# Talking-heads attention and FNet mixing on one core: a new timetable for the mixing stage, and two small copies on another engine

## The chip, the cores and the metric

The kernel runs on one core of one Trainium2 chip. The core has TensorE (in profiles PE, and PEld for its weight loads), VectorE (DVE), ScalarE (ACT), GpSimd (POOL) and SyncE (SP), which issues transfers alone; 16 DMA engines carry the transfers of all queues. What counts is the device time of one launch, in microseconds; the median of several runs is given.

## The reference

Eight batches, twelve heads, 448 rows of 64 numbers a head, all in fp32. Attention comes first, with two small matrices that mix the heads, one before the softmax and one after it:

```python
scores = scale * np.matmul(q, k.transpose(0, 1, 3, 2))
scores = np.einsum('bhij,hg->bgij', scores, w_pre)
scores = scores - np.max(scores, axis=-1, keepdims=True)
attn = np.exp(scores)
attn = attn / (np.sum(attn, axis=-1, keepdims=True) + 1e-09)
attn = np.einsum('bhij,hg->bgij', attn, w_post)
out = np.matmul(attn, v)                        # to x: (8, 448, 768)
X = np.fft.fft(np.fft.fft(x, axis=1), axis=2)
u = x + np.real(X)
un = (u - mean(u)) / np.sqrt(var(u) + 1e-06)    # over the last axis
y = u + np.maximum(un @ w_ch1, 0.0) @ w_ch2     # 768 -> 3072 -> 768
```

## The kernel before

There are two stages: the mixing stage (`mix_phase`), which takes the first 850 us or so and ends with u in device memory, and the dense stage (`ffn_phase`), which normalises u and multiplies it by the two weight matrices. The change lies in the mixing stage alone. The dense stage starts with work of the first batch while the last transform products of the last batch are still open (`parts`).

**Steps.** The rows of a batch are cut into eight blocks (`BLOCKS`), and a block into 3 steps (one has 2), 23 steps a batch (`GS`), 184 in all. In a step twenty rows of all twelve heads go through the softmax. Its work is spread over time: the gather of step T (L493), four transfers on SP that bring rows of scores from the tile Sb into the tile Kr, is written out four steps ahead of T; the product that mixes heads ahead of the softmax, *premix* (L504, out of Kr into the PSUM tiles mx0 and mx1), the maxima (L511, VectorE), the exponentials (L518, ScalarE, out of mx into PP), the reciprocal (L525, L526) and the scaling (L528, POOL) two steps ahead; the product that mixes heads after it, *postmix* (L538, into po), and its transposition, *turn* (L551, VectorE, into Pv), in step T itself. mx0 and mx1 have one buffer each, Kr and PP three.

**Products that fill the steps.** Beside these fixed parts TensorE has other products, which a timetable spreads over the steps:

- T: transposition of q or k for a third of the heads (L450); Tq0 is that of q's third 0. It needs two score banks, emptied by ScalarE and VectorE, one each.
- QK: the scores of one block, for a third of the heads (L476); QK3.1 is block 3, third 1. Two banks, emptied by ScalarE into Sb (L342).
- AV: attention times v for two blocks (a group of rows) and a third of the heads (L568). Two banks, emptied by ScalarE into the tile XT (L342), in four small copies each.
- X: transposition of a group's result (L612), two banks, emptied by ScalarE into the tile X; X0 to X3 are the four groups.
- z: four products of the transform along rows (L677), z0 to z3, one bank each, ScalarE.
- s: four products of the transform along columns (L693), s00, s01, s10, s11 (pair of groups, parity), one bank each; VectorE adds each to X in four additions (L704, L706). After s01 and s11 the pair's rows are stored: by an indirect transfer that POOL issues (L716) and by plain ones on SP (L722, L724). L722 writes into the same tensor as the indirect one and waits until that has landed.

The score banks are a ring of four PSUM tiles, ms (`pms`, L336), shared by all products of the list; mx has two banks and po two. Between X and z lie the *folds* (L633 to L655), twenty pieces of elementwise work a batch on POOL, of which one or two are dealt out in a step.

**Rows that straddle.** Two groups of rows don't end where the transform's groups end, so a few columns of XT are copied to another group's XT (`SPILL`, L594): 15 columns of group 3 to group 1, 7 of group 2 to group 3, for six pieces each. This is done straight after the last eviction of an AV (inside `done`), and X of the receiving group has to wait for it. In the kernel before, POOL makes these copies.

**The timetable.** The constants `AT_*` say in which step of a batch (counted from the batch's first, so over 22 means during the next batch) a product is due: AT_T for T, by third of heads and q or k, counted one batch back; AT_QK for QK, counted from 7 steps ahead of the block; AT_AV for AV, counted from the group's last step plus one; AT_X, AT_Z and AT_S for X, z and s. AT_L and AT_V are the steps of the loads of q, k and v, which POOL issues; the loads of q and k are given out in the order in which the transpositions are due. Below, *place* is the number of a step within a batch, 0 to 22, and T, z, s and X of another batch are meant where the batch in question has none due at that place.

**Order within a step.** The main loop (L808 to L840) takes the parts of a step in one of two written orders, the first in even steps and the second in odd ones; as 23 is odd, a place has the other order in the next batch.

```python
ORDERS = tuple(o.split() for o in (
    "conv pre post flush AV max0 exp0 "
    "QK max1 exp1 turn scale full gather",
    "pre post flush max0 max1 QK exp0 "
    "AV turn exp1 scale gather conv full flush"))
```

`full` takes T, X, z and s; `conv` is one step of the conversion of weights for the dense stage (VectorE); `flush` writes out the evictions that are pending. Where a QK or AV would bring more than four pending evictions, and ahead of each product of `full`, they are flushed first. The order on TensorE, VectorE, ScalarE and POOL is kept as written (`manual_schedule`); each engine works through its queue in that order. Only SP's queue is put in order by the scheduler.

Of the kernel before, what the change touches and what calls it, by code (L numbers as in the profile page):

```python
# [85 lines left out]

AT_T = ((5, 9), (16, 17), (13, 15))
AT_L = ((-4, -3), (-2, -1), (0, 1), (2, 7), (11, 12), (13, 14))  # L90
AT_V = ((3, 4), (5, 6), (7, 7))
AT_QK = ((1, 2, 2), (0, 1, 2), (0, 1, 2), (1, 1, 2),
         (0, 1, 2), (0, 1, 2), (0, 1, 2), (0, 1, 2))
AT_AV = ((1, 2, 3), (0, 1, 5), (3, 4, 5), (1, 2, 4))
AT_X = ((11, 0), (23, 1), (28, 3), (30, 2))
AT_Z = (39, 39, 41, 41)
AT_S = ((40, 44), (46, 50))

ORDERS = tuple(o.split() for o in (
    "conv pre post flush AV max0 exp0 "  # L100
# [47 lines left out]
def _ap(t: bass.AP, offset: int, dims) -> bass.AP:  # L148
    return bass.AP(tensor=t.tensor, offset=t.offset + offset,
                   ap=[list(d) for d in dims])  # L150
# [6 lines left out]
def _row(t: bass.AP) -> int:  # L157
    return t.ap[0][0]
# [144 lines left out]
def mix_phase(ctx, tc, rest, ident, q, k, v, w_pre, w_post, u_scr, u_rev, wts):  # L303
# [6 lines left out]
    nc = tc.nc  # L310
# [30 lines left out]
    def copy(eng, out, in_):  # L341
        (nc.scalar.copy if eng == "a" else nc.vector.tensor_copy)(out=out, in_=in_)  # L342
# [11 lines left out]
    def ms_tile():  # L354
        return ms[-1]()
# [41 lines left out]
    first = {}  # L397
    START = sorted(range(3), key=lambda xx: max(AT_T[xx]))
    blocks = [dict(b=n // NBL, r0=BLOCKS[n % NBL][0], rs=BLOCKS[n % NBL][1])
# [7 lines left out]
    def emit_load_qk(b, xx, nm, y):  # L407

        src = q if nm == "q" else k
        if y == 0 and b == 0 and xx == START[-1]:  # L410

            if "raw" not in first:
                first["raw"] = ppv.tile([P, GT, 2 * S], F32, name="Pv", tag="Pv")
            batches[b]["raw" + nm, xx] = first["raw"][:, nm == "q"].rearrange(
                "p (c x d) -> p c x d", c=C7, x=2)
        elif y == 0:
            batches[b]["raw" + nm, xx] = praw.tile([P, C7, 2, D], F32, name="raw" + nm,
                                                   tag="raw")
        t = batches[b]["raw" + nm, xx]
        for x in range(2):  # L420
            eng = nc.gpsimd if b else (nc.sync, nc.scalar)[x]
            eng.dma_start(
                out=t[64 * y:64 * y + 64, :, x, :],
                in_=src[b, 6 * y + 2 * xx + x].rearrange("(p c) d -> p c d", c=C7))
        return True
# [36 lines left out]
    def emit_qk(n, xx):  # L462

        bk = blocks[n]
        st = batches[bk["b"]]
        if "Sb" not in bk:
            bk["Sb"] = psb.tile([P, 6, S], F32, name="Sb", tag="Sb")
        c0, w = bk["r0"] + MG, R * bk["rs"]
        n = 64 + w
        pss = [ms_tile() for _ in range(2)]  # L470
        for y in range(2):
            for o in (64 * y, 64 * y + 32):
                lo = c0 + o - 64 + (0 if y else w)
                hi = min(lo + 32, c0 + w)
                for x in range(2):
                    nc.tensor.matmul(  # L476
                        pss[x][o:o + hi - lo, :S],
                        st["qT", xx][64 * x:64 * x + 64, y, lo:hi],
                        st["kT", xx][64 * x:64 * x + 64, y, :],
                        start=True, stop=True)  # L480
        return [lambda x=x: copy(ENG["QK"][x], bk["Sb"][:n, 2 * xx + x, :],
                                 pss[x][:n, :S]) for x in range(2)]
# [73 lines left out]
    def emit_av(a, pr):  # L556

        b, k = divmod(a, NG)
        st = batches[b]
        Pv = turned[a]["Pv"]  # L560
        rp = _row(Pv)
        nu = (GROUP_AT[k + 1] - GROUP_AT[k]) * 4
        pss = [ms_tile() for _ in range(2)]
        for jb in range(C7):
            for x in range(2):
                for y in range(2):
                    i = 2 * pr + x
                    nc.tensor.matmul(  # L568
                        pss[y][64 * x:64 * x + 64, :nu * R],
                        st["v", pr][64 * y:64 * y + 64, x, jb * D:(jb + 1) * D],  # L570
                        _ap(Pv, 64 * y * rp + 32 * jb + R * i,
                            [[rp, 64], [HS, nu], [1, R]]),
                        start=(jb == 0), stop=(jb == C7 - 1))
        g = groups[b * NG + BLOCKS[2 * k][3]]
        if pr == 0:
            g["XT"] = pxt.tile([P, 6, XW], F32, name="XT", tag="XT")
        XT = g["XT"]
        rx = _row(XT)

        def done(y):  # L580
            rs = _row(pss[y])
            c = 0
            for _, w, n, _, first, sg in BLOCKS[2 * k:2 * k + 2]:
                dst = _ap(XT, (3 * y + pr) * XW + PG[g["gi"]] + first,
                          [[rx, P], [sg * w, R], [sg, w]])
                src = _ap(pss[y], c, [[rs, P], [1, R], [R, w]])
                copy(ENG["AV"][y], dst, src)
                c += R * w
            if y == 1 and pr == 2:
                if k in SPILL:  # L590
                    gi, c0, n, go, co = SPILL[k]
                    Xo = groups[b * NG + go]["XT"]
                    back = -1 if gi == 2 else 1
                    nc.gpsimd.tensor_copy(  # L594
                        out=_ap(Xo, PG[go] + co, [[rx, P], [XW, 6], [1 - 2 * (go == 1), n]]),
                        in_=_ap(XT, PG[gi] + c0, [[rx, P], [XW, 6], [back, n]]))
                if k in NONE:
                    gi, cols = NONE[k]
                    for o in cols:
                        Xo = groups[b * NG + gi]["XT"]  # L600
                        nc.vector.memset(Xo[:, :, PG[gi] + o:PG[gi] + o + 1], 0.0)
        return [lambda y=y: done(y) for y in range(2)]

    def emit_x(g):
        X = pxx.tile([PN, DM], F32, name="X", tag="X")
        XT, p0 = g.pop("XT"), PG[g["gi"]]
        g["X"] = X
        evs = []
        for u in range(2):
            ps = ms_tile()  # L610
            for i in range(3):
                nc.tensor.transpose(ps[:PN, i * P:(i + 1) * P],  # L612
                                    XT[:, 3 * u + i, p0:p0 + PN], ident[:, :])
            evs.append(lambda u=u, ps=ps: copy(ENG["X"][u], X[:, u * DH:(u + 1) * DH],
                                               ps[:PN, :DH]))
        if g["gi"] in (1, 2):
            fold(g)
        return evs
# [113 lines left out]
    def due(kind, at, fn):  # L732
        fill[kind].append((at, len(fill[kind]), fn))
# [4 lines left out]
    for b in range(B):  # L738
        f = b * GS
        at_t = [(a, nm, xx) for xx, at in enumerate(AT_T) for nm, a in zip("qk", at)]  # L740
        if b == 0:
# [11 lines left out]
        else:  # L753
            for at, (a, nm, xx) in zip(AT_L, sorted(at_t, key=lambda e: e[0])):
                for y in range(2):
                    due("none", f + at[y] - GS,
                        lambda b=b, xx=xx, nm=nm, y=y: emit_load_qk(b, xx, nm, y))
            for xx, at in enumerate(AT_T):
                for nm, a in zip("qk", at):
# [5 lines left out]
        for n in range(0 if b else 2, NBL):  # L765
            for xx in range(3):
                due("QK", f + BLOCK_AT[n] - 7 + AT_QK[n][xx],
                    lambda n=NBL * b + n, xx=xx: (emit_qk(n, xx), n))
        for n in range(NG):
            for pr in range(3):  # L770
                due("AV", f + GROUP_AT[n + 1] + AT_AV[n][pr],
                    lambda a=b * NG + n, pr=pr: (emit_av(a, pr), None))
            at, gi = AT_X[n]
            due("full", f + at, lambda g=groups[b * NG + gi]: emit_x(g))
        for n, at in enumerate(AT_Z):
            due("full", f + at, lambda b=b, n=n: emit_z(b, n // 2, n % 2))
        for pair in range(2):
            for par in range(2):
                due("full", f + AT_S[pair][par],
                    lambda b=b, pair=pair, par=par: emit_s2(b, pair, par))  # L780
# [26 lines left out]
    with tc.manual_schedule(engines={ET.PE, ET.DVE, ET.Activation, ET.Pool}):  # L807
        while s <= TOT - GS + AT_X[-1][0]:  # L808
            old = len(later)
# [592 lines left out]
```

## Time and profile before

| what | value |
|---|---|
| time, median of 3 runs | 2429.42 us (2429.25 to 2429.75) |
| the profiled execution: its own time, its span | 2420.56 us, 2418.7 us |
| TensorE busy, whole span | 2307.4 us, 95% |
| VectorE, ScalarE, GpSimd busy, whole span | 71%, 46%, 47% |
| premix (L504), postmix (L538), QK (L476), busy | 234.6, 211.3, 208.5 us |
| AV (L568), busy | 161.7 us |
| maxima (L511), exponentials (L518), scaling (L528), busy | 215.2, 230.6, 239.3 us |
| the straddling copies on POOL (L594) | 16, of 0.255 us at the median |
| from 840 to 910 us, between the stages | TensorE idle for about half of it |

The busy time of TensorE is that of overlapping instructions with modelled ends, so it says how little is idle, not how near the engine is to its peak. More is told by the waits, and by the distance from one group of products to the next on TensorE's timeline: a group that comes at the usual distance was not held up. fp32 products show twice in the records (16 for the eight of a premix). A wait is put down to the semaphore that came last.

### The profile page before, as it was taken

The numbers are of one execution on the slowest core, as the hardware profiler recorded it, in microseconds if no ns is written. First come the engines' busy times: TensorE is split into PE (matmuls) and PEld (weight loads), VectorE is DVE, ScalarE is ACT, GpSimd is POOL, SyncE is SP. The second block draws the span as 40 slices with busy tenths as digits, with TensorE's granted clock in tenths as the row PEclk, the third lists the DMA queues.
The fourth block names the chain that finished last, engine by engine and source line by source line (L and its number), as shares of the span: only waits on it lengthen the run. The fifth ranks groups of instructions, "written<-read, shape, count | busy, mean of one in ns | idle before, by whom it ended". The sixth has DMA issues, their size and how long they took to land.

```text
span 2418.7 us, 59291 instructions
## 1 busy us (share of the span) xinstructions
PE 2307.4 (95%) x22600; PEld 1726.4 (71%) x22600; DVE 1706.3 (71%) x3596; ACT 1106.3 (46%) x3069; POOL 1133.5 (47%) x1684
## 2 busy tenths in 40 slices
PE   6999999999999949999999999999999999999998
PEld 3445454554545437676777779999899999999998
DVE  3878778777877735778576776777776777776546
ACT  4766666665666622323122224344444444444444
POOL 3577867766785651121043344333433343344333
PEclk9999999999999979999999999999999999999999
DMA  7555555645554473574887895657565756575553
GB/s 164 162 163 168 164 161 154 178 151 166 172 167 138 155 237 126 177 230 167 307 206 223 243 277 159 181 145 240 151 168 148 227 151 188 144 220 126 144 124 66
DMA packets 213384, 425.59 MB, mean 176 GB/s; under 512 B 38766, under 2 KB 135430, under 8 KB 213102
## 3 DMA queue, kind: packets, MB, share of 16 engines
q1 hardware_dynamic: 142446, 280.38, 33.4%
q0 software_dynamic: 64656, 139.45, 26.6%
q8 instruction: 181, 2.97, 0.5%
q10 hardware_dynamic: 6000, 1.97, 0.4%
q14 instruction: 101, 0.83, 0.1%
HBM read 213.16 MB, written 129.39 MB: 142 GB/s over the span
## 4 chain that ended last, share of the span: by engine, by line
PE 73%; issue 7%; DVE 6%; POOL 6%; DMA 4%; ACT 3%; SPq 1%; ACTq 0%; POOLq 0%; DVEq 0%
PE psP L1058 15%; PE psP L1188 10%; PE psR L1058 8%; PE mx L504 5%; PE psR L1188 5%; PE ms L568 5%; PE psQ L1058 4%; PE psP L1131 4%; PE ms L476 4%; PE po L538 4%; PE psQ L1188 2%; DMA Kr<-Sb 2%; PE psR L1131 2%; PE ms L693 2%; ACT PP L518 1%
## 5 line engine op out<-in xcount | busy, mean ns | idle before, releaser
L1058 PE MATMUL psP<-ub,w1t 128*128 128x256 f32 x2016 | 480.5, 379 | 1.2 <-DVE h L1077 1.2
L1058 PEld LDWEIGHTS psP<-ub,w1t 128*128 128x128 f32 x2016 | 379.0, 190 | 49.5 <-DVE h L1077 1.6
L528 POOL TENSOR_SCALAR PP<-PP,rcp 128x448 f32<-128x448 f32 x368 | 239.3, 659 | 255.7 <-DVE rcp L526 218.6
L518 ACT ACTIVATE PP<-mx,nmx 128x448 f32<-128x448 f32 x368 | 230.6, 631 | 217.9 <-DVE nmx L511 203.8
L511 DVE TENSOR_REDUCE nmx<-mx 128x1 f32<-128x448 f32 x368 | 215.2, 618 | 104.0 <-PE mx L504 101.5
L1222 POOL DMA_DIRECT2D out_dram<-od x109 | 132.9, 1394 | 280.0 <-DVE od L1219 157.6
L504 PE MATMUL mx<-Kr,kw 60*32 60x448 f32 x2944 | 234.6, 559 | 22.2 <-ACT PP L518 13.0
L1022 POOL TENSOR_TENSOR hq<-h 128x256 f32<-128x256 f32 (+1 forms) x168 | 104.1, 620 | 295.3 <-ACT h L1078 174.1
L1058 PE MATMUL psR<-ub,w1t 128*128 128x256 f32 x1008 | 232.5, 380 | 0.0
L1219 DVE TENSOR_TENSOR od<-od 128x768 f32<-128x768 f32 x196 | 188.9, 975 | 52.4 <-ACT od L1216 50.6
L476 PE MATMUL ms<-kT,qT 64*32 64x448 f32 (+2 forms) x3072 | 208.5, 544 | 8.3 <-ACT qT L342 6.3
L538 PE MATMUL po<-PP,kw 60*32 60x448 f32 x2944 | 211.3, 542 | 1.4 <-POOL PP L528 1.4
L1058 PEld LDWEIGHTS psR<-ub,w1t 128*128 128x128 f32 x1008 | 192.4, 191 | 26.3
L551 DVE STREAM_TRANSPOSE Pv<-po 128x896 f32<-128x896 f32 x184 | 203.9, 1108 | 9.9 <-PE po L538 7.8
L342 ACT COPY Sb<-ms 124x448 f32<-124x448 f32 (+1 forms) x384 | 184.5, 540 | 27.8 <-PE ms L476 22.6
L1216 ACT COPY od<-psP 128x192 f32<-128x192 f32 x390 | 124.7, 320 | 145.8 <-PE psP L1188 141.3
L568 PEld LDWEIGHTS ms<-Pv,vv 64*64 64x64 f32 x5376 | 138.4, 132 | 71.1 <-issue 47.9
L225 POOL DMA_DIRECT2D raw<-in_moe_w_ch_dram x88 | 53.5, 608 | 270.6 <-DVE tmp L269 253.3
L568 PE MATMUL ms<-Pv,vv 64*64 64x120 f32 (+1 forms) x5376 | 161.7, 263 | 0.8 <-issue 0.6
L1131 PE MATMUL psP<-w2t,h 128*128 128x384 f32 x448 | 153.7, 486 | 0.0
L504 PEld LDWEIGHTS mx<-Kr,kw 60*32 60x32 f32 x2944 | 48.1, 106 | 124.1 <-ACT PP L518 74.3
L1077 DVE TENSOR_TENSOR h<-h,psP 128x512 f32<-128x512 f32 x42 | 28.9, 687 | 143.4 <-PE psP L1058 143.1
(142 smaller groups left out, 4577.5 us busy)
## 6 DMA issues: line engine op xcount, KB each, us to landing
ub<-ub SPq DMA_DIRECT2D x294, 384.0 KB
Kr<-Sb SPq DMA_DIRECT2D x736, 105.0 KB
out_dram<-od POOLq DMA_DIRECT2D x137, 384.0 KB, 7.8
w1t<-w SPq DMA_DIRECT2D x42, 384.0 KB
w2t<-w SPq DMA_DIRECT2D x42, 384.0 KB
raw<-in_moe_w_ch_dram POOLq DMA_DIRECT2D x56, 256.0 KB, 3.8
raw<-in_moe_w_ch_dram POOLq DMA_DIRECT2D x32, 384.0 KB, 4.9
w<-wst POOLq DMA_DIRECT2D x92, 128.0 KB, 4.6
```

The lines of the kernel that those rows point to most:

```text
L476: nc.tensor.matmul(pss[x][o:o + hi - lo, :S], st["qT", xx][64 * x:64 * x + 64, y, lo:hi], st["kT", xx][64 * x:64 * x + 64, y, :], start=Tr ...
L504: nc.tensor.matmul(mx[x][64 * z + o:64 * z + o + 32, :S], kw1[64 * x:64 * x + KR, o:o + 32], Kr[64 * x:64 * x + KR, z, :], start=True, sto ...
L511: nc.vector.tensor_reduce(nmx[:, :], steps[T]["mx"][x][:, :S], axis=AX.X, op=ALU.max, negate=True)
L518: nc.scalar.activation(steps[T]["PP"][:, x, :], steps[T]["mx"][x][:, :S], ACTF.Exp, bias=steps[T]["nmx", x][:, :], accum_out=steps[T]["den ...
L528: nc.gpsimd.tensor_scalar(PP[:, x, :], PP[:, x, :], rcp[:, x:x + 1], 1.0, op0=ALU.mult, op1=ALU.mult)
L538: nc.tensor.matmul(po[o:o + 32, z, :S], kw2[64 * z:64 * z + KR, y, :], PP[64 * z:64 * z + KR, :, c * HS:(c + 1) * HS], start=True, stop=True)
L551: nc.vector.transpose(turned[a]["Pv"][:, j, :].rearrange("p (z s) -> p z s", z=2), steps[T]["po"][:, :, :S])
L568: nc.tensor.matmul(pss[y][64 * x:64 * x + 64, :nu * R], st["v", pr][64 * y:64 * y + 64, x, jb * D:(jb + 1) * D], _ap(Pv, 64 * y * rp + 32 ...
L1058: nc.tensor.matmul(p[:, m, :], w1[i][:, kc, m * P:(m + 1) * P], ub[:, kc, :], start=i in (0, 4, 1)[:3 - seed] and m == kc == 0, stop=kc == ...
L1131: nc.tensor.matmul(p, h[:, LHS[i], kf, x * P:(x + 1) * P], w2[i][:, kf, :], start=i in (0, 4, 1)[:3 - (c > 0)] and kf == 0, stop=kf == FM ...
L1188: nc.tensor.matmul(ps[j, key][:, :DQ], a, b, start=m in (0, 4), stop=True, skip_group_check=True)
L1219: eng.tensor_tensor(D[j][:, :, :], D[j][:, :, :], D[k][:, :, :], op=ALU.add)
```

## The change

The timetable gets other numbers, and ScalarE makes the straddling copies instead of POOL. Nothing is computed otherwise, and the number of products, copies and transfers stays the same. By place within a batch, the moves are:

- QK3.1 from 2 to 3; s11 from 4 to 3; X2 from 7 to 6
- AV0.2 from 9 to 10; X0 from 11 to 13; AV1.2 from 16 to 14; Tq1 from 16 to 15
- QK0.0 of the next batch from 17 to 16, QK0.2 of it from 18 to 17 (QK0.1 stays at 18)
- AV2.0 from 20 to 18, AV2.1 from 21 to 20; z2 and z3 from 18 to 19
- the loads of q's third 1 and of k's third 2 change places (2 and 7 against 11 and 12), as their transpositions do
- the loop has one step less after the last batch, as it ends with X2

On SP the row store L722 of pair 1 stands two gathers' worth of steps earlier in every second batch (before the gather for place 10 of the even batches, where it was before that for place 12), and at the same point in the others. In the last batches' tail s11 comes ahead of AV3.2 instead of behind it.

```diff
-AT_T = ((5, 9), (16, 17), (13, 15))
+AT_T = ((5, 9), (15, 17), (13, 15))
 AT_L = ((-4, -3), (-2, -1), (0, 1), (2, 7), (11, 12), (13, 14))
 AT_V = ((3, 4), (5, 6), (7, 7))
-AT_QK = ((1, 2, 2), (0, 1, 2), (0, 1, 2), (1, 1, 2),
+AT_QK = ((0, 2, 1), (0, 1, 2), (0, 1, 2), (1, 2, 2),
          (0, 1, 2), (0, 1, 2), (0, 1, 2), (0, 1, 2))
-AT_AV = ((1, 2, 3), (0, 1, 5), (3, 4, 5), (1, 2, 4))
-AT_X = ((11, 0), (23, 1), (28, 3), (30, 2))
-AT_Z = (39, 39, 41, 41)
-AT_S = ((40, 44), (46, 50))
+AT_AV = ((1, 2, 4), (0, 1, 3), (1, 3, 5), (1, 2, 4))
+AT_X = ((13, 0), (23, 1), (28, 3), (29, 2))
+AT_Z = (39, 39, 42, 42)
+AT_S = ((40, 44), (46, 49))
...
-                    nc.gpsimd.tensor_copy(
+                    nc.scalar.copy(
                         out=_ap(Xo, PG[go] + co, [[rx, P], [XW, 6], [1 - 2 * (go == 1), n]]),
                         in_=_ap(XT, PG[gi] + c0, [[rx, P], [XW, 6], [back, n]]))
```

## The prediction

> **What bounds the kernel now.** I read the page first: all edits lie in the mixing stage, the first 850 us of the span of 2418.7 us. Then the busy time of two whole batches of 23 steps, one whose first step takes the even order of work (batch 2) and one that takes the odd (batch 3); columns: length, then PE, PEld, DVE, ACT, POOL busy (instructions), clock, DMA share, GB/s.
>
> ```profile
> 232.31:335.94 103.63, 99.33 (x1926) 54.37 (x1926) 80.01 (x166) 68.18 (x206) 79.23 (x123) 1.00 0.53 163
> 335.94:441.81 105.87, 100.25 (x1931) 54.12 (x1919) 82.36 (x164) 68.32 (x209) 76.67 (x119) 1.00 0.54 163
> ```
>
> TensorE is busy 95% of it, and its work is the same after the change; so only its waits can go or come. Their list for 60 to 860 us (total, times, longest):
>
> ```profile
> PE mx L504 <- ACT PP L518: 12.1, 19, 2.6
> PE ms L612 <- POOL XT L594: 11.1, 10, 2.7
> PE ms L677 <- ACT Sb L342: 4.6, 6, 1.0
> PE ms L450 <- ACT Sb L342: 3.7, 3, 1.4
> PE mx L504 <- DMA Kr<-Sb: 3.1, 6, 1.2
> ```
>
> The first is the softmax chain in steps that hold too few products; the second is the copy that the change moves; the next two are score banks not yet emptied; the last is a gather. The timeline of PE shows where. A step runs from one premix (L504, 16 records) to the next, and undisturbed groups follow each other at fixed distances: premix 0.78, postmix 0.75 (0.89 ahead of an AV), QK 0.75 to 0.9, AV 1.63 (1.4 if short), a transposition 0.9, an s product 1.4 to 1.5. Lines of three places in batches 2 and 3:
>
> ```profile
> 296.66 0.96 PE L476 MATMUL ms<-kT,qT 64*32 64x448 f32 x16
> 298.67 1.24 PE L504 MATMUL mx<-Kr,kw 60*32 60x448 f32 x12 [1.05 <-ACT PP L518]
> ...
> 317.42 1.79 PE L677 MATMUL ms<-ts,xf 112*96 112x113 f32 x16 [0.89 <-ACT Sb L342]
> ...
> 363.08 0.91 PE L612 MATMUL ms<-ident,XT 128*113 128x128 f32 x6 [0.54 <-POOL XT L594]
> 365.40 0.98 PE L450 MATMUL ms<-ident,rawq 128*128 128x128 f32 x7 [1.41 <-ACT Sb L342]
> ```
>
> Place 14 (one QK only) waits 1.05 for the exponentials. Place 18 (two QKs, then z2 and z3) waits 0.89 for the first QK's bank. Place 5 waits for the copy, then 1.41 more for a bank: had the copy been early, the bank would have held it as long. VectorE tells why that bank was late: the four additions of s11 stood ahead of the maxima.
>
> ```profile
> 361.56 0.55 DVE L706 TENSOR_TENSOR X<-X,ms 113x383 f32<-113x383 f32 x1
> 362.03 0.92 DVE L273 TENSOR_TENSOR wst<-wst,tmp 128x256 f32<-128x256 f32 x1
> 362.88 1.14 DVE L511 TENSOR_REDUCE nmx<-mx 128x1 f32<-128x448 f32 x2
> ```
>
> **What the Trainium skill says.** Its page "PSUM — Partial Sum Buffer" (Specifications) gives 8 banks a partition, of 512 fp32 values. The kernel takes two for mx, two for po, four for ms: the ring of four can't grow, and the trace shows its waits (4.6 + 3.7 us). "Perfetto Trace Analysis" (Tensor Engine Instruction) says that ACT, DVE and GPSIMD are strict FIFO; the POOL copy, behind scalings, folds and loads, agrees: its own 0.26 us is preceded by PE waits of up to 2.7. "DMA: Bandwidth & Descriptors" (Issuing engines are not separate DMA queues) says all queues share 16 engines; the trace has a gather on the chain that took 7.18 us from 268.05, while V and k loads ran.
>
> **The change part by part.** Step lengths before are from PE's timeline of batch 2 / 3.
>
> *Copies.* 16 copies leave POOL (0.26 us at the median) for ScalarE, straight behind the evictions that they read. No row shows that form; bounds are 0.20 (128x40, XT) and 0.50 (113x384, X). On the line between 128x60 (0.226) and 113x384 (0.495) 90 and 42 elements cost 0.25 and 0.21: 0.46 a batch, hidden in ScalarE's 35% idle time; uncovered it would be 3.7 us over 8 batches. Queued behind the copy are evictions of a QK or exponentials, 0.25 late, and VectorE's memset of the same tile (L601), with the maxima behind it. VectorE spends 3.2 us a step (two maxima 1.24, turn 1.11, reciprocal 0.34, a weight conversion some 0.5), so steps of over 4 us cover that. Gained: in odd batches the wait ahead of X1 at place 0 (1.0 in batches 3 and 5, 0.4 in batch 1), all of it; at place 5 next to nothing (bank), but in batch 7, which has no transposition there, 2 to 3.
>
> *Places 2 to 7* (QK3.1 from 2 to 3; s11 from 4 to 3; X2 from 7 to 6). Before: 4.83+3.05+6.35+5.41+3.05+5.95 = 28.6 / 5.25+2.66+6.16+6.25+2.52+5.93 = 28.8. After: 2 and 4 become QK+AV (4.05 to 4.65 in their like: 4.1, 4.5), 3 two QKs with s11: 4.66 of work plus a bank wait as at place 18 (0.7) = 5.4; 5 stays 5.3, the additions being gone and the bank wait not; 6 becomes 3.4, X2 filling a light step; 7 is QK+AV, 4.6. Sum 27.3: gain 1.3 / 1.5.
>
> *Places 9 to 21* (AV0.2 to 10, X0 to 13, AV1.2 to 14, Tq1 to 15, QK0.0 to 16, QK0.2 to 17, AV2.0 to 18, z2 and z3 to 19, AV2.1 to 20). Before 57.6 in batch 2 and 58.9 in batch 3. After: 9 is 4.2 (its gather stays late: it is issued on the eviction of QK4.2, and steps 7 and 8 are now 8.7 instead of 10), 10 and 11 4.5, 12 3.8, 13 and 15 5.1 each (4.2 of work, 0.9 for QK's bank), 14 4.3, 16 and 19 4.4, 17 4.7, 18 4.5, 20 4.6, 21 4.1: 58.2: 0.6 lost in batch 2, 0.7 gained in 3. The waits of light steps become bank waits. Of the dearer cases of batches 4 to 6 (place 14 5.13, 15 5.32, 9 6.77 and 8.31) I count half as saved, by my choice: steps of over 4 us cover VectorE. Two waits are new. Tq1 at 15 clears its pads on POOL (L444, L445, 0.1 each) once QK7.2 of that step has read the old buffer; scalings stand behind them, needed two steps later: free. QK0.0's eviction at 16 overwrites the scores of block 6, one step earlier than before, so it waits for the last gather from them; that is issued behind the premix of place 14, takes SP 3.2 and lands some 2 later, some 4 us ahead of the eviction: free.
>
> *Loads and queues.* q1 and k2 change places in POOL's loads: k2 now has 3 steps (13 us) from issue to use; such loads land in 2.7 to 5.7 us. Free. In even batches the stores of pair 1 are issued two steps earlier; on SP the row store L722, which waits 2.5 to 4.6 us for the indirect store, stands before the gather of place 8 instead of 10. The gathers behind it are late by that; they were issued some 8 us ahead of their use, so I take 0, bounds 0 and 2 us in three batches.
>
> *Sum.* Even batches: 1.3 - 0.6, and 0.3 at place 1 (4.6 becomes 4.3), 1.0 x 3; half of what 4 and 6 take more than 2 (106.5 and 105.2 against 103.6), 2.2: 5.2. Odd: 1.5 + 0.7 + 1.0 (copy) = 3.2 in batch 3; 4.4 in 5 (half of the 2.4 that it takes more); batch 1, which has neither s10 nor s11, 2.5 in the same way (27.4 - 25.2 at 2 to 7, -0.1 at 9 to 21, 0.4 copy): 10.1. Batch 0, AVs moved alone: 1, estimated. Batch 7: 3 at place 5. Tail: the last s11 (861.16) moves ahead of one of three AVs (4.95 us together): 1.6; the store that begins at 864.27 heads the chain to the second stage's loads. Total 20.9; I round it down to 20, as new waits are likelier to be missed than new gains. Against the profiled execution's span: 2418.7 - 20 = 2398.7. It took 2420.56, and the median is 2429.42, 8.9 above; the same step gives **2409.4**.
>
> **Rivals.** *Better:* all light-step waits go and the banks cost nothing: 0.9 less at places 3, 13 and 15 in 7 batches, 19 more: 2390. For: 12.1 us of waits for exponentials. Against: place 18's wait shows in all six batches.
> *Nothing:* places 2 to 7 give only 0.5, and dear batches stay dear: 7 x 0.5 = 3.5, copies and tail 2.4 + 2.5 + 1.6: about 2419; with gathers late by 2 us in three even batches 2425. For: the place-by-place sum of 9 to 21, near nothing.
> *Slower, by the ring of four ms banks:* places 3, 13 and 15 each ask for more than four banks, so the last product waits for a QK eviction behind both exponentials. I priced this 0.7 to 0.9. Place 5, built alike, ran 6.25 to 7.27 in odd batches with 4.1 of work. If each of the three costs 1.5 more than priced, 31 us are lost in 7 batches: 2440. It decides from 0.95 more (20/7/3). Against: place 5 had VectorE late by s11, and 13 and 15 have no additions; but 15 gives VectorE 1.67 us of evictions, and 17 follows with 2.2 of additions and 0.55.
>
> **How the numbers follow.** Forecast (2400 to 2420) 0.55; better 0.12; nothing 0.15; slower 0.18. Within 0.2% is 2424.6 to 2434.3, about what a measurement of this kernel can tell from no change. Of "nothing" half is faster than that; of "slower" a sixth lies inside. Faster 0.55+0.12+0.07 = 0.74, same 0.11, slower 0.15. Range 2394 to 2436: it leaves out most of the slower case and the end of the better one; the forecast's own range is 2400 to 2420.
>
> **What would show it.** Right: no PE wait on POOL XT; place 14 over 4 us with no wait for PP; place 13 near 5.1 with T waiting for Sb; batches of 101 to 104 us; the store of the tail at about 862 minus the stage's gain. Wrong: place 3, 13 or 15 above 6; premix at place 8 or 9 waiting for Kr in every even batch; VectorE behind at 18, so that premix waits for PP there.

## The result, and the profile after

| | median | runs |
|---|---|---|
| before | 2429.34 us | 6 runs, 2420.45 to 2430.75 |
| after | 2389.08 us | 6 runs, 2381.97 to 2394.12 |

The ratio is 0.9836, interval 0.9814 to 0.9858: 40 us less, twice the forecast of 20 and 5 us below the range. Single slow executions (of the kernel before 2488.72 us, and of one variant 9237.21) are left out of every ratio below. The profiled execution took 2391.53 us, with a span of 2389.8. TensorE's busy time stays near what it was (2291.4 us; 2307.4 before). The same two batches as in the prediction, from the first premix of each to the next (columns as there: length, PE, PEld, DVE, ACT, POOL, clock, DMA share, GB/s):

```profile
229.44:328.97 99.53, 97.02 (x1926) 53.65 (x1926) 85.15 (x166) 66.67 (x207) 78.88 (x121) 0.98 0.56 169
328.97:430.97 102.00, 97.28 (x1931) 52.58 (x1919) 81.05 (x164) 67.50 (x211) 76.40 (x118) 0.98 0.57 169
```

They are 4.1 and 3.9 us shorter than before. PE's busy time fell by 2.3 and 3.0 of that, with the same work, so some of what counted as busy had been waiting. And the clock is 0.98, where it was 1.00: there is something new in them. PE's waits from 60 to 860 us (one of 19.5 us that belongs to the dense stage is left out):

```profile
PE mx L504 <- DMA Kr<-Sb: 9.9, 8, 3.2
PE mx L504 <- ACT PP L518: 6.6, 5, 2.0
PE ms L450 <- ACT Sb L342: 5.2, 13, 1.4
PE ms L693 <- ACT Sb L342: 1.9, 6, 0.3
PE ms L612 <- ACT XT L594: 0.8, 1, 0.8
```

The copy's wait went (11.1 to 0.8), as forecast, and the waits for score banks are small. The wait for a gather grew from 3.1 to 9.9 us, which was not forecast. PE's timeline has the places that the prediction showed: 13, with X0 and two transpositions behind one QK; 18 to 20 of batch 2; 5 of batch 3.

```profile
289.19 0.91 PE L612 MATMUL ms<-ident,XT 128*113 128x128 f32 x6
290.34 0.98 PE L450 MATMUL ms<-ident,rawq 128*128 128x128 f32 x7 [0.23 <-ACT Sb L342]
...
316.89 0.98 PE L504 MATMUL mx<-Kr,kw 60*32 60x448 f32 x16
317.67 0.96 PE L538 MATMUL po<-PP,kw 60*32 60x448 f32 x16
318.56 1.71 PE L568 MATMUL ms<-Pv,vv 64*64 64x120 f32 x56
320.20 0.98 PE L476 MATMUL ms<-kT,qT 64*32 64x448 f32 x16
320.98 0.96 PE L504 MATMUL mx<-Kr,kw 60*32 60x448 f32 x16
...
355.44 0.98 PE L450 MATMUL ms<-ident,rawq 128*128 128x128 f32 x7 [0.63 <-ACT Sb L342]
```

The bank at place 13 costs 0.23 where 0.9 was priced; place 5 keeps half of its bank wait. Place 20 (316.89 to 320.98), with one QK and one AV, is 4.09 long, the plain sum of its four groups: 0.78 + 0.89 + 1.64 + 0.78. The step of the same kind before the change, which had served as the price, looked like this on PE's timeline of batch 2:

```profile
321.66 1.20 PE L504 MATMUL mx<-Kr,kw 60*32 60x448 f32 x12
322.49 0.60 PE L538 MATMUL po<-PP,kw 60*32 60x448 f32 x4
322.68 0.56 PE L504 MATMUL mx<-Kr,kw 60*32 60x448 f32 x4
322.86 1.12 PE L538 MATMUL po<-PP,kw 60*32 60x448 f32 x12
323.91 1.70 PE L568 MATMUL ms<-Pv,vv 64*64 64x120 f32 x56
325.54 0.98 PE L476 MATMUL ms<-kT,qT 64*32 64x448 f32 x16
326.32 0.96 PE L504 MATMUL mx<-Kr,kw 60*32 60x448 f32 x16
```

It is 4.66 long, and no wait is printed. Yet from the first premix record to the AV it takes 2.25 us, where after it takes 1.67: the premix comes in pieces (12 records, then 4 between those of the postmix) behind a step of 2.52. The trace has the reason on ScalarE: the exponentials of the step before end at 321.51 and 322.13, and the premix, which overwrites both banks, starts the records of its two halves at 321.66 and 322.28. A light step's wait had gone into the length of the next one.

The new stalls are two. In batches 3 and 5 place 9 takes 9.33 and 11.12 us, where its groups alone make 3.3 (as in batch 6 of the variant with the row stored apart, 3.31). "Place 9's gather" is the one that brings the rows which the premix at place 9 reads. PE's lines in batch 3, and SP's queue at that time:

```profile
367.71 0.94 PE L504 MATMUL mx<-Kr,kw 60*32 60x448 f32 x4
371.86 1.82 PE L504 MATMUL mx<-Kr,kw 60*32 60x448 f32 x10 [3.21 <-DMA Kr<-Sb]
```

```profile
351.00 7.15 SPq L493 DMA_DIRECT2D Kr<-Sb  x8
362.53 0.23 SPq L722 DMA_DIRECT2D v<-X  x1
362.86 7.39 SPq L493 DMA_DIRECT2D Kr<-Sb  x9
```

SP had issued place 8's gather by 358.15, then stood at the row store L722 for the indirect store, and issued place 9's gather from 362.86 to 366.09; the premix could go on at 371.86. So the gather was issued late, and its transfer took long besides. The wait printed is 3.21 us (3.10 in batch 5; the expectations below say 4.4 and 5.3); much of the rest is the clock, which was 0.50 from 371.42 to 374.84, and in batch 5 from 572.81 to 579.64. In even batches place 6 waits for the exponentials, and place 7 runs at half clock. PE, VectorE and POOL in batch 2:

```profile
258.14 0.91 PE L612 MATMUL ms<-ident,XT 128*113 128x128 f32 x6
260.97 1.20 PE L504 MATMUL mx<-Kr,kw 60*32 60x448 f32 x12 [1.93 <-ACT PP L518]
```

```profile
254.44 2.15 DVE L525 TENSOR_SCALAR rcp<-den 128x2 f32<-128x2 f32 x1
...
257.83 1.74 DVE L255 TENSOR_SCALAR wst<-tmp 128x256 uint32<-128x256 uint32 x1
259.49 1.14 DVE L511 TENSOR_REDUCE nmx<-mx 128x1 f32<-128x448 f32 x2
```

```profile
254.57 1.97 POOL L633 TENSOR_TENSOR xs<-X 113x384 f32<-113x384 f32 x2
```

```profile
262.20:265.60 3.40, 3.40 (x36) 1.17 (x20) 2.26 (x5) 2.20 (x7) 3.40 (x6) 0.50 0.72 161
```

The addition of 1e-9 to two columns, 0.17 us at the median, took 2.15 while POOL folded, and the weight conversion L255 took 1.74; the maxima behind them came late, then the exponentials; and after 1.93 us without a product TensorE's clock was 0.50 for 3.40 us (the last fence: the same columns as the batches above).

### The profile page after: what moved, and what is told of

The parts are those of the page before. It is cut to its first block, busy times and chain, and to the rows that moved or that the text cites. A ratio compares the mean times of both kernels' runs of the same rounds, so it can differ in the third digit from the quotient of the medians.

```text
span 2389.8 us, 59344 instructions
## 1 busy us (share of the span) xinstructions
PE 2291.4 (96%) x22600; PEld 1721.5 (72%) x22600; DVE 1706.5 (71%) x3596; ACT 1101.2 (46%) x3085; POOL 1132.6 (47%) x1668
## 3 DMA queue, kind: packets, MB, share of 16 engines
q10 hardware_dynamic: 6000, 1.97, 0.5%
## 4 chain that ended last, share of the span: by engine, by line
PE 57%; issue 3%; POOL 2%; DVE 2%; DMA 1%; ACT 0%; SPq 0%; POOLq 0%; DVEq 0%
PE psP L1058 16%; PE psP L1188 10%; PE psR L1058 9%; PE psP L1131 5%; PE psR L1188 5%; PE psQ L1058 4%; PE psR L1131 3%; PE psQ L1188 2%; PE psQ L1131 1%; PE psQ L992 1%; DVE hq L1022 0%; DMA u<-u 0%; POOL w L233 0%; DMA w<-wst 0%; POOL xs L633 0%
## 5 line engine op out<-in xcount | busy, mean ns | idle before, releaser
L504 PE MATMUL mx<-Kr,kw 60*32 60x448 f32 x2944 | 218.7, 555 | 23.7 <-DMA Kr<-Sb 16.2
L476 PE MATMUL ms<-kT,qT 64*32 64x448 f32 (+1 forms) x3072 | 208.7, 555 | 7.9 <-ACT qT L342 6.5
L538 PE MATMUL po<-PP,kw 60*32 60x448 f32 x2944 | 202.4, 548 | 0.2 <-POOL PP L528 0.2
L568 PEld LDWEIGHTS ms<-Pv,vv 64*64 64x64 f32 x5376 | 137.0, 132 | 71.2 <-issue 57.0
L568 PE MATMUL ms<-Pv,vv 64*64 64x120 f32 (+1 forms) x5376 | 158.7, 263 | 0.6 <-ACT X L342 0.6
L476 PEld LDWEIGHTS ms<-kT,qT 64*32 64x32 f32 (+2 forms) x3072 | 64.8, 107 | 80.9 <-issue 54.9
```

The costliest lines, as they stand in the source:

```text
L476: nc.tensor.matmul(pss[x][o:o + hi - lo, :S], st["qT", xx][64 * x:64 * x + 64, y, lo:hi], st["kT", xx][64 * x:64 * x + 64, y, :], start=Tr ...
L504: nc.tensor.matmul(mx[x][64 * z + o:64 * z + o + 32, :S], kw1[64 * x:64 * x + KR, o:o + 32], Kr[64 * x:64 * x + KR, z, :], start=True, sto ...
L538: nc.tensor.matmul(po[o:o + 32, z, :S], kw2[64 * z:64 * z + KR, y, :], PP[64 * z:64 * z + KR, :, c * HS:(c + 1) * HS], start=True, stop=True)
L568: nc.tensor.matmul(pss[y][64 * x:64 * x + 64, :nu * R], st["v", pr][64 * y:64 * y + 64, x, jb * D:(jb + 1) * D], _ap(Pv, 64 * y * rp + 32 ...
```

## The experiments

All ratios are to the kernel before, run on the same chip beside the variant (9 to 36 runs of it each, medians of 2425.3 to 2428.6 us; 4 to 20 runs of a variant); 0.001 is 2.4 us. "Copies alone" is the base of the partial timetables.

| kernel | median us | ratio, interval |
|---|---|---|
| copies alone | 2423.01 | 0.9972, 0.9959 to 0.9985 |
| timetable alone | 2397.72 | 0.9864, 0.9827 to 0.9900 |
| copies + places 2 to 7 | 2418.02 | 0.9956, 0.9943 to 0.9970 |
| copies + places 18 to 21 | 2415.53 | 0.9949, 0.9935 to 0.9962 |
| copies + places 9 to 16 | 2409.34 | 0.9932, 0.9909 to 0.9955 |
| copies + places 9 to 21 | 2398.14 | 0.9870, 0.9834 to 0.9905 |

**The copies, with the old timetable.** The L594 line of the change's diff alone, on the kernel before.

> The kernel before with only the two copies of straddling rows moved from GpSimd to ScalarE; the old timetable stays. Theory (the timetable carries the change): the copies free only the premix of place 0 in odd batches and the last batch's X1, about -5 us (1.0 + 1.0 + 0.4 + 2 to 3). Rival (the copies carry it, because VectorE and GpSimd get in each other's way): -20 us or more. Rival (copies on ScalarE delay the exponentials behind them): 0 to +10 us.

Measured: 6.8 us by the ratio, near the theory's 5; both rivals fell. The copies on ScalarE took 0.247 us at the median, as priced (0.46 for the two), and PE's wait for XT fell from 11.1 to 0.4.

**The timetable, with the old copies.** The kernel after, with

```diff
-                    nc.scalar.copy(
+                    nc.gpsimd.tensor_copy(
```

> The kernel after with the two copies put back on GpSimd; the new timetable alone. Theory (the timetable carries the change): 2429 - 40 + about 5 to 8 = 2394 to 2397 us. Rival (the copies carry it): 2409 us or above.

The timetable gives 33 us by itself (2397.72 us, just above the theory's range, far from the rival's 2409), about five sixths of the change. The copies' 6.8 on top of it is the difference of two ratios whose intervals touch, so that it equals their worth alone is not shown; the traces show that they are still worth something. With POOL's copies PE's waits for them come to 21.4 us in 9, and place 5 of even batches takes 7.7 to 9.4 us; with ScalarE's it takes 4.5, but place 6, which takes 3.3 to 4.3 with POOL's copies, takes 5.3 to 5.4.

**The timetable by places.** Each on top of the copies alone:

```diff
 places 2 to 7
-AT_QK = ((1, 2, 2), ..., (1, 1, 2), ...   AT_X = (..., (30, 2))   AT_S = (..., (46, 50))
+AT_QK = ((1, 2, 2), ..., (1, 2, 2), ...   AT_X = (..., (29, 2))   AT_S = (..., (46, 49))
 places 9 to 21
+AT_T = (..., (15, 17), ...)   AT_QK = ((0, 2, 1), ...   AT_X = ((13, 0), ...
+AT_AV = ((1, 2, 4), (0, 1, 3), (1, 3, 5), (1, 2, 4))   AT_Z = (39, 39, 42, 42)
 places 18 to 21: of these only AT_AV[2] = (1, 3, 5) and AT_Z
 places 9 to 16:  of these only AT_AV[0], AT_AV[1], AT_X and AT_T
```

> The kernel before with the copies on ScalarE and only the part of the new timetable that lies in places 2 to 7: attention steps of slot 3 as (1, 2, 2), Xf.X of group 2 at 29, its S at 49. Theory after the traces (the gain lies in places 9 to 21, while what places 2 to 7 gain in odd batches goes into the stall of place 9 and in even batches into the stall of place 6): 0 to -5 us against the copies alone. Rival (the prediction's own accounting, +1.3 to 1.5 a batch): -10 us against the copies alone.

> The kernel before with the copies on ScalarE and only the part of the new timetable that lies in places 9 to 21: T of group 1 at 15, attention steps of slot 0 as (0, 2, 1), new AV steps, Xf.X of group 0 at 13, Z at 42. Theory after the traces (attention steps run at TensorE's own length, 4.05 us, with bank waits of 0.3): 4 to 5 us in each of 6 batches, -25 to -35 us against the kernel before. Rival (the prediction's accounting: -0.6 to +0.7 a batch): -5 us against the kernel before, that is, no more than the copies.

> The kernel before with the copies on ScalarE and only the edits of places 18 to 21: AV steps of group 2 as (1, 3, 5), the last two Z at 42. Each of the four steps then holds as much as the next. Theory (a step with one attention product and one more runs at the sum of its groups, 0.78 + 0.89 + 0.75 + 1.63 = 4.05 us, and every light or crowded step pays for its unevenness): 19.0 us in places 18 to 21 become 16.3, about 2.5 a batch, -17 to -20 us against the copies alone. Rival (the prediction's prices, 4.5 + 4.4 + 4.6 + 4.1 = 17.6): -8 to -10 us. Rival (it is in places 9 to 17 that the new timetable gains): under -6 us.

> The kernel before with the copies on ScalarE and only the edits of places 9 to 16: AV steps of groups 0 and 1 as (1, 2, 4) and (0, 1, 3), Xf.X of group 0 at 13, T of q1 at 15. Theory (attention steps at the sum of their groups, 4.05 us or less, bank waits 0.3): places 9 to 16 fall from 34.0 us in batch 2 to about 32.4, and more where place 9 or 14 was dear: -10 to -17 us against the copies alone; with places 18 to 21 alone at -6, the two edits of slot 0's steps, which neither has, are then worth little. Rival (the prediction's prices: 31.5 for places 9 to 15 and 3.6 for place 16): +5 to +8 us against the copies alone. Rival (no group of places carries the gain by itself, only all moves together): 0 to -6 us.

Against the copies alone: places 2 to 7 give 3.9 us, 9 to 21 give 24.8, of which 18 to 21 alone 5.6 and 9 to 16 alone 9.7. So the first two theories held. Of those on the halves, that on 18 to 21 fell, as they carry no 17 to 20 us; 9 to 16 came out at the lower end of theirs (10 to 17), within the noise. Step lengths in the profiles tell why (mean of batches 2, 4 and 6; sums of the distances between premixes):

| | places 2 to 7 | 9 to 21 | of these 18 to 21 | place 9, batches 3 and 5 |
|---|---|---|---|---|
| copies alone | 29.3 | 60.5 | 19.0 | 7.1 |
| + 2 to 7 | 28.4 | 60.0 | 19.0 | 11.6 |
| + 18 to 21 | 28.9 | 59.2 | 18.1 | 7.6 |
| + 9 to 16 | 29.4 | 57.6 | 19.2 | 6.6 |
| + 9 to 21 | 28.9 | 56.0 | 16.3 | 5.1 |
| after | 29.5 | 54.0 | 16.3 | 10.2 |

With 18 to 21 alone, QK0.2 stays in place 18, which then holds two QKs and an AV (4.82), and 19 has a QK, z2 and z3 (5.31): the step at 20, no longer behind a light one, reaches its plain length (4.08, from 4.66), and 21, with one AV less, takes 3.88 in place of 5.52; but the sum falls by only 0.9. It takes the move of QK0.2 to 17 (the first entry of AT_QK, which is in neither half) to empty 18: some 9 of the 24.8 us come only with all moves together (the intervals of these kernels are 5 to 9 us to either side of 10 and 25, so this remainder is rough; the step lengths are firmer). Places 2 to 7 show the stall of place 9 as it arises: in batches 3 and 5 they shorten from 29.7 to 25.7, and place 9 grows from 7.1 to 11.6. PE's waits of that kernel:

```profile
PE mx L504 <- DMA Kr<-Sb: 13.7, 8, 4.7
PE mx L504 <- ACT PP L518: 10.5, 10, 2.2
```

**The held-up addition (place 6).** The kernels after and before, with

```diff
-        nc.vector.tensor_scalar(rcp[:, :], den[:, :], 1e-9, None, op0=ALU.add)
-        nc.vector.reciprocal(out=rcp[:, :], in_=rcp[:, :])
+        nc.vector.reciprocal(out=rcp[:, :], in_=den[:, :])
```

> The kernel after without the addition of 1e-9 to the softmax's denominators (VectorE, 128 x 2, 0.13 to 0.17 us where undisturbed, 2.15 us at 254.44 beside GpSimd's folds); this small part of the computation is left out, the reciprocal reads the sums themselves. Theory (VectorE held up by GpSimd's folds sets the stall of 1.9 us at place 6 of the even batches, and the clock's dip at place 7 follows from it with about 1.7): -5 to -12 us against the kernel after. Rival (the reciprocal behind it takes over the wait, as it reads the same buffer at the same moment): 0 to -3 us.

> The same small addition left out of the kernel before. Theory (the hold-up of VectorE is a cost that the new timetable met at place 6, while the old one ran into it elsewhere or had slack): 0 to -6 us against the kernel before, less than what the same edit gives the kernel after. Rival (the hold-ups cost both timetables alike): the same as in the kernel after, within 2 us.

After: 2390.07 us, 0.9843 (0.9809 to 0.9877), no gain that shows, though four runs do not exclude the theory's 5 us; before: 2420.61, 0.9977 (0.9962 to 0.9991), 5.6 us. The first theory was not borne out as to the time, and the rivals' reasons fell. The reciprocal took over nothing: it never exceeded 0.17 us in 177 places. In the kernel after, places 2 to 7 of even batches fell from 29.5 to 26.5, but place 8 rose from 4.1 to 5.7 and 9 from 4.1 to 4.7, waiting for their gathers; and place 7 ran at the full clock in all three (4.6 in place of 6.3). VectorE shows that the hold-up itself went to the next instruction of that sort, behind the reciprocal, where the chain no longer ran through it (POOL's two folds ran from 253.21 to 255.19):

```profile
253.38 0.17 DVE L525 RECIPROCAL rcp<-den 128x2 f32<-128x2 f32 x1
253.46 1.88 DVE L251 TENSOR_SCALAR tmp<-tmp 128x256 f32<-128x256 f32 x1
```

**The row store, issued later.** On the kernel after, the store of L722 was put off by three steps in the program; then with the addition left out as well.

```diff
+        def row(n, X):
+            if n:
+                later.append(lambda: row(n - 1, X))
+            else:
+                nc.sync.dma_start(out=u_rev[b][GR:GR + 1, :], in_=X[GR:GR + 1, :])
...
-                        nc.sync.dma_start(out=u_rev[b][GR:GR + 1, :], in_=X[GR:GR + 1, :])
+                        row(3, X)
```

> The kernel after with the store of the X row (L722, SP's queue) issued three steps later, so that SP no longer stands at it while place 9's gather of Kr waits behind. Theory (the store held SP's queue until the rows' indirect store was done, and made the gather late at place 9 of odd batches, 4.4 and 5.3 us of wait in batches 3 and 5, with a half clock after it): -8 to -14 us against the kernel after, and no wait for Kr over 2 us at place 9. Rival (the gather is late because of its own transfer on busy DMA queues): 0 to -2 us, the wait for Kr stays.

> Both edits on the kernel after: the row's store three steps later, and the addition of 1e-9 left out. Theory (the two stalls lie in different batches and add up): -13 to -25 us against the kernel after, 2364 to 2376 us. Rival (the stall only moves: what is gained in one batch is waited for in the next, as gathers or loads come no earlier): -8 us or less.

2387.55 us (0.9825, 0.9789 to 0.9862) and 2388.28 (0.9836, 0.9803 to 0.9870): no gain that shows. But these two tell nothing of the row store: on SP it still stood directly ahead of place 9's gather (SP's order is not that of the program text), and waited as long, 31.4 and 32.1 us in 7 waits each.

**One indirect store of 113 rows.** It takes the row store away altogether:

```diff
-                            ap=rows[:GR, pair:pair + 1], axis=0),
-                        in_=X[:GR, :], in_offset=None)
-                    if pair:
-                        nc.sync.dma_start(out=u_rev[b][GR:GR + 1, :], in_=X[GR:GR + 1, :])
+                            ap=rows[:GR + pair, pair:pair + 1], axis=0),
+                        in_=X[:GR + pair, :], in_offset=None)
```

> The kernel after with the row store L722 gone from SP: the indirect store of pair 1 writes all 113 rows, so SP waits for nothing of it and place 9's gather can be issued when its score block is ready. (Issued three steps later the row store still stood directly before that gather on SP, so that run could not tell.) Theory (the row store's wait, 28 us in 7 waits on SP, makes place 9's gather late): the gather of place 9 in batches 3 and 5 is issued 3 us or more earlier, the premix behind it waits under 2 us instead of 4.4 and 5.3, and 8 to 16 us are gained against the kernel after. Rival (the gather waits for the block's scores or for its own slow transfer): under 3 us.

> The same with the addition of 1e-9 left out as well. Without the addition alone the stall of place 6 went (5.3 to 4.15 us a step) and place 8 became 1.6 longer, waiting for its gather: the stall moved. Theory (that gather was late by the row store): place 8 falls back to 4.1, and both edits give 16 to 28 us against the kernel after, 2361 to 2373 us. Rival (gathers are late by themselves): 2385 us or above.

> The kernel before with the one indirect store. Theory (the old timetable met the late gather as well, at places 9 of batches 4, 5 and 6, 6.8 to 8.3 us in place of 5.8): -3 to -8 us against the kernel before. Rival (it is the new timetable alone that runs into it): 0 to -2 us.

All three were slower: 2453.31 us (1.0098, 1.0068 to 1.0127), 2450.70 (1.0085, 1.0054 to 1.0117), and on the kernel before 2513.52 (1.0350, 1.0320 to 1.0380). The page's list of DMAs (median us from issue to landing at the end) has the indirect stores at 4.7 us in the kernel after and the V loads, which follow them in POOL's queue, at 4.3. With 113 rows:

```profile
vv<-in_v_dram POOLq DMA_DIRECT2D x42, 224.0 KB, 14.4
v<-X,rows POOLq DMA_INDIRECT x16, 21.6
```

The 16 stores are those of both pairs, and only three landings are on record here: 21.6 and 22.3 us with 113 rows, 4.4 with 112. The AVs waited for V ("PE ms L568 <- DMA vv<-in_v_dram", 65.0 us in 9 waits), 16 to 20 us in place 8. The Trainium skill's page "DMA: Bandwidth & Descriptors" (Why a DMA increments its semaphore by 16 and not by 1) says that a transfer is spread over the largest number of engines up to 16 that divides the slowest dimension on both of its sides, with an exception for some direct copies that GpSimd issues; it does not speak of indirect ones. If the rule holds for them, 112 rows get 16 engines and the prime 113 gets 1. The landing times point that way, though no run here shows the engines of that transfer. The theory was thus covered by a cost of the experiment itself; what it showed was that place 9's gather in batch 3 now came 2.6 us behind place 8's, instead of 4.7.

**The row, stored apart.** Row 112 of the other buffer is written by nothing, so the row can go there and need not wait:

```diff
-ENDS = (GR, GR * 2 + 1, GR * 3 + 1, S)
+ENDS = (GR + 1, GR * 2 + 1, GR * 3 + 1, S)
...
-                        nc.sync.dma_start(out=u_rev[b][GR:GR + 1, :], in_=X[GR:GR + 1, :])
+                        nc.sync.dma_start(out=u_scr[b][GR:GR + 1, :], in_=X[GR:GR + 1, :])
```

> The kernel after with the row of L722 stored to row 112 of the other buffer (u), which nothing else writes, and read from there by the second stage (ENDS begins with GR + 1): SP no longer waits for the indirect store, which keeps its 112 rows. Theory (that wait is a part of the stall of place 9): the gather of place 9 is issued about 2 us earlier in batches 3 and 5 (with the one store of 113 rows it came 2.5 to 2.6 us behind the one before it, instead of 4.6 to 4.7), the premix waits 0 to 2.5 us instead of 4.4 and 5.3, and -3 to -8 us against the kernel after. Rival (SP only waits for the block's scores in its place): 0 to -2 us.

> The same, with the addition of 1e-9 to the denominators left out as well. Theory (the stall of place 6 moved to place 8, to a gather that the row store made late): places 6 to 8 of even batches take 13.0 instead of 15.7 us, -8 to -16 us against the kernel after, 2373 to 2381 us. Rival (gathers at places 8 and 9 are late by their own issue and landing): -5 us or less.

> The kernel before with the row stored apart in the same way. Theory (the old timetable's steps 5 to 8 were longer, and the gather nearly in time): 0 to -4 us against the kernel before. Rival (both timetables lose the same by it): as much as in the kernel after, within 1 us.

On the kernel after: 2379.98 us, 0.9808 (0.9782 to 0.9835). SP's queue and PE at place 9 of batch 3:

```profile
351.30 14.81 SPq L493 DMA_DIRECT2D Kr<-Sb  x16
```

```profile
367.11 1.20 PE L504 MATMUL mx<-Kr,kw 60*32 60x448 f32 x16
...
372.09 1.36 PE L504 MATMUL mx<-Kr,kw 60*32 60x448 f32 x10 [0.49 <-DMA Kr<-Sb]
```

No store stands between the gathers now: place 9's is issued from 359.62 on, 1.8 us behind the end of place 8's (2.5 in batch 5), where it was 4.7 (4.6), and its premix at 367.11 has no wait. Place 9 of batches 3 and 5 takes 4.4 us on average instead of 10.2, without a fall of the clock. A part moves on: place 10 waits 0.5 for its own gather and takes 6.3 and 5.8 instead of 4.1. These batches take 99.2 instead of 102.8. With the addition left out as well: 2380.04 us, 0.9807 (0.9778 to 0.9836), nothing more: places 2 to 7 of even batches are 1.8 us shorter, but place 9 takes 0.8 of it back and batches 3 and 5 are 2 us longer. On the kernel before the row stored apart gives nothing: 2431.12 us, 1.0015 (1.0000 to 1.0030). There place 9 (5.0 us by its groups, as in batch 0) took 6.4 and 8.3 us in batches 3 and 5 and takes 6.1 and 7.7 with the row apart, so the store held up little: with its longer steps SP issued that gather 7.9 us ahead of its premix in batch 3, where after the change it was 4.9. What else makes place 9 long there stays open. The kernel after and its variant ran once more on one chip:

> The kernel after once more, on the same chip as its variant with the row stored apart. Theory (the stall of place 9 is SP's wait for the indirect store): 8 to 12 us above the variant. Rival (the two ratios of before, 0.984 and 0.981, differ by chance): within 3 us of it.

> The variant with the row stored apart, beside the kernel after. Theory: 8 to 12 us below it, about 2380 us. Rival: within 3 us of it.

2389.33 us (0.9839, 0.9816 to 0.9862) and 2381.30 (0.9810, 0.9790 to 0.9830): 8.0 us, the lower end of the theory. The ranges of the five runs each overlap by less than 1 us (2382.8 to 2394.3 and 2377.7 to 2383.6), so the difference is clear of chance and its size rough. The traces repeat it too: place 9 of batches 3 and 5 takes 10.0 and 4.9 us, and PE's waits for gathers come to 8.4 and 4.8.

## Why the prediction was wrong, point by point

The direction was right, the size was half. Between the two profiled executions the miss is 9 us (spans 2418.7 to 2389.8, against 2398.7 forecast); the other 11 lie in how these two executions stand to their medians.

**The offset: wrong.** The prediction set the median 8.9 above the profiled execution for both kernels. The execution of before was a low draw of a wide spread, that of after lies 2.4 above its own median. The spread goes with the granted clock: in 36 runs of the kernel before beside the first experiments, 2421.4 to 2437.7 us, those with a mean clock of 0.984 took 2434.6 on average (6 runs) and those with 0.987 took 2427.4 (9 runs), 2.4 us for 0.001 of it, which is what 0.001 of the whole time comes to. One profiled execution was no base to 10 us, and three runs within 0.5 us of each other did not show the spread.

**Copies: right.** Forecast 5.4 (1.0 + 1.0 + 0.4, and 3 in batch 7), measured 6.8 (3.6 to 10) with the old timetable; where the waits went is as forecast (place 0 of batches 3 and 5 fell from 5.97 to 4.72 and 4.78, place 5 of batch 7 from 6.37 to 3.46, place 5 of batch 3 stayed).

**Places 9 to 21: the step that failed.** "After: 9 is 4.2 ..., 10 and 11 4.5, 12 3.8, 13 and 15 5.1 each ...: 58.2." In even batches it is 54.0 in place of 58.2. The prices of QK+AV steps, "4.05 to 4.65 in their like", made 22.4 for places 10, 11, 14, 18 and 20, and they took 20.1; the banks, 0.9 each at 13 and 15, cost 0.25 and 0.4 over the 4.2 of work, and the two places took 9.1 in place of 10.2; 16, 17 and 19 took 0.4 less, and 21 (a QK and s01) 0.2. The upper prices were read off steps that stood behind a light one and held its wait inside, as the pieces of the premix at 321.66 show; the run with places 18 to 21 alone bears it out, where place 20 has no light step ahead of it and takes 4.08. The sum of the prediction's own distances, 0.78 + 0.89 + 1.63 + 0.75 = 4.05, was the price. The runs measured 24.8 us for these places, where the prediction had some 3 (-0.5 by the places, and half of the dear batches). The dear cases were not halved but gone (places 14 and 15 of batch 4, 5.13 and 5.32, took 3.86 and 4.46).

**Places 2 to 7: half right.** Forecast 27.3. Odd batches took 25.5 (the bank at place 3 cost 0.32, where 0.7 was priced; 6 and 7 ran at 3.3 and 4.1), even ones 29.5, with the stall of place 6 and the half clock of 7. The prediction took VectorE's addition and reciprocal at their undisturbed 0.34 in every step, though the kernel before has the same hold-ups (the addition L525 takes 46.8 us in all from 60 to 850 us, 177 times, where 0.16 each would be 28).

**The gather of place 9: "9 is 4.2 (its gather stays late ...)" was the second failure.** The text had the cause in its hands, steps 7 and 8 shorter by 1.3 and a gather that comes late, and priced it at some 0.9 (4.2, where the groups of place 9 make 3.3), about what it had been late before (1.0 in batch 2); it took 5 to 7 us more in each of batches 3 and 5, the clock's fall included. That the shorter steps bring it on is shown by places 2 to 7 alone (7.1 to 11.6). The row stored apart wins back 3.6 and 4.2 of it, place 10 counted in; the rest stays as waits for gathers at places 9 and 10. The prediction counted the row store only for even batches, where it is earlier now and where 0 was about right (99.9 us a batch without it, 100.4 with it); it cost where it had not moved, because the steps ahead of it had become shorter.

**Rivals.** "Better" gave 2390, and the time was 2389, but by chance: banks at places 3, 13 and 15 gave 1.5 us a batch of the 2.7 that it needed, the attention steps gave what it did not count on, and two stalls that it did not know took some of it back. "Slower" by the ring of four banks is refuted: from batch 1 on the places 3, 13 and 15 stayed at 5.1 or less. Of the signs, no wait for POOL's copy came true, and place 14 lost its wait (it is 3.8 to 4.2 long, not over 4); 13 at 5.1 did not. None of the signs of being wrong showed, and they missed both stalls: a premix did wait long at place 9, but in odd batches.

**What stays open.** That VectorE was held up by POOL's folds is read from their times: in the kernel after all nine additions of over 0.5 us end 0.02 to 0.04 us behind the end of a POOL instruction (eight folds and one scaling), and of 139 that ran beside no POOL work none took over 0.42. It agrees with what the Trainium skill's "GPSIMD Engine Reference" (1. Specifications) says: POOL's interfaces to SBUF are shared with VectorE, with contention for VectorE instructions in a two-port mode or with two SBUF inputs. The addition and the conversions stretched while the reciprocal did not; the folds were not taken away in any run, and in which mode these instructions ran no trace shows. Why place 9's transfer took long once issued (5.8 us from the end of its issue to the premix) stays open too, as does why the 113 rows cost the kernel before more than the kernel after (85 against 64 us).

## What to carry to other kernels

Price a step by the sum of its groups' own distances, and suspect a wait in every longer step of the trace, even where no wait is printed: look for a group that comes in pieces. A timetable that makes steps shorter brings forward the use of everything that is issued at a fixed point behind another transfer, so look for the transfers with the least time in hand and for what stands ahead of them on their queue, also where the change doesn't move them. And set a forecast against several executions, not one, when its gain is of the size of their spread.

## What the runs showed of the hardware

- A VectorE addition on 128x2 values took 2.15 us in place of 0.17 beside two POOL operations of 1.97 us together; the reciprocal of the same size was never held up (0.17 at most in 184).
- TensorE's clock fell to 0.50 on a fixed grid of times. In the profile of the kernel after the falls between 60 and 800 us begin at 262.20, 371.42, 463.58, 572.81 and 668.38, that is 32, 59, 91 and 119 times 3.413 us behind the first, and they last 3.41 us, one of them 6.83. In the 3.41 us of the grid ahead of each, products took 0.64 to 1.49 us; in every piece that no half clock followed they took 2.0 or more. The Trainium skill's "TensorE: Matmul & The Clock Gate" (Part 1: The HAM clock gate) gives an idle window of about 3.4 us, free-running. The grid agrees; but the window need not be idle, it had up to 1.49 us of products. Other runs have pieces of 1.5 to 2.0 us with a fall behind them and without, so the limit is not sharp.
- So the same stall of 2 us cost 1.7 us more where it fell into one piece of the grid, and nothing more where it straddled two. With the row's store issued later in the program place 6 of batch 2 was as long (5.27 us; 5.25 in the kernel after), but the piece of the grid at its stall held 1.96 us of products, no half clock followed, and place 7 took 4.6 us instead of 6.3.
- An indirect store of 113 rows of 3 KB landed in 21.6 to 23.8 us (twelve on record in the three kernels that have it), one of 112 rows in the same kernels in 3.6 to 5.8 (six).
